# Attention scores on the tensor engine: one 64 x 128 tile per product in place of four 64 x 32 tiles

## The chip, the cores and the metric

The kernel runs on one core of a Trainium2 chip. The metric is the device time of one execution in microseconds (us), lower is better. A TensorE product ("matmul") holds one operand still in the array (its weights, brought in by a separate weight load) and streams the other past it, up to 512 columns, into a bank of PSUM. The array can be divided into tiles, so that several small products run at once.

## The reference

```
q, k, v = (x @ wqkv) split into 32 heads of 16     # x is 2048 x 512, bf16
scores  = q @ k.T / 4 ;  p = softmax(scores)       # 32 heads x 2048 x 2048
a       = (p @ v, heads joined) @ wo
b       = ((x @ w_gate) * (x @ w_up)) @ w_down     # inner width 1376
g       = sigmoid(sum(x * gate_w))
out     = g * a + (1 - g) * b
```

## The kernel before, in words

A host-side planner (`_Sched`) walks simulated time and writes out the instruction order of every engine by hand; `_Plan.emit` then adds the semaphores. Nothing is decided on the chip: each engine works through its list in order.

TensorE is used as two halves, array rows 0 to 63 (r = 0) and 64 to 127 (r = 1). The unit of work is a **group**, `pe64`: up to four matmuls of 64 rows x 32 columns side by side (`tile_position=(64 * r, 32 * cc)`, cc = 0 to 3), which together fill one half and stream the same 512 columns of time into one PSUM bank. The planner charges each group 0.216 us on its half (`s_a`, `s_d`, `v_job`, the default `slot` of `_Unit`) and picks for the two halves separately in `try_pe` and `pe_phase`, so that groups of the two halves run side by side. There are three kinds of group:

- **Scores** (`scores`, called from `s_a` and `s_d`): for one chunk of 512 queries and one block of 128 keys, the 128 keys are the weights (`KT`) and the masked queries (`QM`) are streamed. Four matmuls have the same streamed operand and differ in their 32 keys and their 32 PSUM rows. 2,048 groups, 8,192 matmuls.
- **P times V** (`pv`, from `v_job`): the weights are V of four different heads, 16 columns and a column of ones each (17), and each of the four matmuls streams another head's exponentials. 2,092 groups; these can't be one tile, as each column strip has its own streamed operand.
- **Fills** (`fill`): projections for q, k, v, the gate and up products, the down and output products, and the gate's row. 1,576 groups, nearly all of four matmuls.

ScalarE takes the exponentials of some score banks (`exp`, L1671), VectorE does others by an integer approximation (`dpass`, L1710), and VectorE and GpSimd make scaled copies of those (`copy`, L1716 and L1717). Matmuls, evacuations and copies of several (query, key) steps are in flight together, in eight PSUM banks.

Full-array matmuls (128 x 128) come only at the start: seven warm-ups (L1954), transposes of x (L1963 and L1658, the latter from `x_turn`, four matmuls a call), and the first projections (L1978). The calls of `x_turn` lie between score groups; the planner books both halves for 0.6 us for one (`x_full`).

Of the kernel before, what the change touches and what calls it, by code (L numbers as in the profile page):

```python
# [1502 lines left out]
class _Hw:  # L1503
# [63 lines left out]
        self.ps = stack.enter_context(nc.psum_tensor("ps", [128, 8, 512], F32))  # L1567


    def pe64(self, r, mms, deps):  # L1570
        def fn(pe):
            o = None
            for dst, lhs, rhs, st, sp, cc in mms:
                o = pe.matmul(dst, lhs, rhs, start=st, stop=sp, tile_position=(64 * r, 32 * cc), skip_group_check=True)  # L1574
            return o

        return self.P.op("pe", fn, deps, "pe%d" % r)

    def scores(self, r, bank, c, b, s, kt, ci, deps):
        var = s + 2 * (ci % 2)  # L1580
        lo, hi = 64 * r, 64 * r + 64
        q = self.QM[lo:hi, (4 * c + b) % 2, var, :]
        mms = []
        for cc in range(4):
            k0 = kt * 128 + 32 * cc
            mms.append((self.ps[32 * cc : 32 * cc + 32, bank, :], self.KT[lo:hi, b, k0 : k0 + 32], q, True, True, cc))
        return self.pe64(r, mms, deps)

    def cell(self, x, lo, hi):
# [17 lines left out]
    def fill(self, u, r, i, start, stop, deps):  # L1607
        lo, hi = 64 * r, 64 * r + 64
        bank = u.bank
        kind = u.mm[0]  # L1610
        mms = []
        n = 4
        if kind == "gate":
            for cc in range(1, 4) if u.mm[1] else (0,):
                mms.append((self.ps[32 * cc : 32 * cc + 1, bank, :], self.gw[lo:hi, i : i + 1], self.xT[lo:hi, cc, i, :], start, stop, cc))
            return self.pe64(r, mms, deps)
        for cc in range(4):
            c0 = 32 * cc
            if kind in ("k", "q", "u", "g"):
                if kind == "k":  # L1620
                    b, ch = u.mm[1:]
                    w = self.wk[lo:hi, i, 128 * b + c0 : 128 * b + c0 + 32]
                elif kind == "q":
                    ch, b = u.mm[1:]
                    w = self.wq[lo:hi, i, 128 * b + c0 : 128 * b + c0 + 32]
                else:
                    ch, f = u.mm[1:]
                    if c0 >= self.FW[f]:
                        continue
                    w = (self.wu if kind == "u" else self.wg)[lo:hi, i, 128 * f + c0 : 128 * f + c0 + 32]  # L1630
                x = self.xT[lo:hi, ch, i, :]
            elif kind == "v":
                ch, tt = divmod(u.mm[1], 4)
                t0 = 128 * tt + c0
                w, x = self.xT[lo:hi, ch, i, t0 : t0 + 32], self.wv[lo:hi, i, :]
            elif kind == "do":
                c, tt = u.mm[1:]
                t0 = 128 * tt + c0
                if i < 11:
                    w, x = self.hT[lo:hi, i, t0 : t0 + 32], self.wd[lo:hi, i, :]  # L1640
                else:
                    w, x = self.OT[lo:hi, (4 * c + i - 11) % 8, t0 : t0 + 32], self.wo[lo:hi, i - 11, :]
            else:
                t0 = 128 * u.mm[1] + c0
                w = self.OT[lo:hi, (12 + i) % 8, t0 : t0 + 32]
                x = self.wo[lo:hi, i, :] if i < 3 else self.wq[lo:hi, 0, :]
            mms.append((self.ps[c0 : c0 + 32, bank, :], w, x, start, stop, cc))
        return self.pe64(r, mms, deps)


# [531 lines left out]
```

## Time and profile before

| | us |
|---|---|
| median of 3 runs | 699.54 (692.03 to 699.86) |
| profiled execution, its own time | 705.51 |
| its span, first to last instruction | 703.7 |
| PE busy, weight loads busy | 682.0, 393.0 |
| ACT, DVE, POOL busy | 660.0, 624.5, 545.3 |

PE is TensorE's matmuls, PEld its weight loads, DVE VectorE, ACT ScalarE, POOL GpSimd. A row of the groups gives line, engine, operation, output and inputs, shape and count, then the busy time, the mean duration of one in ns, and the idle time before them with what ended it. `64*32 64x512` is a product with weights of 64 rows and 32 columns that streams 512 columns. All groups of four have line 1574, that of `pe64`. The end of a matmul is modelled, so its duration (about 0.38 us) is longer than the time after which the next one can follow; the spacing of the starts tells the throughput. A row of the timeline gives start, length, engine, what it is and how many such instructions were merged into it.

### The profile page before, as it was taken

How to read it: one execution, taken by the hardware profiler on the slowest of the kernel's cores; microseconds unless marked ns; L12 is line 12 of the kernel's file. 1: busy time of each engine (PE TensorE's matmuls, PEld its weight loads, DVE VectorE, ACT ScalarE, POOL GpSimd, SP SyncE). 2: the span in 40 equal slices, each digit the busy share in tenths (PEclk: the TensorE clock that was granted, in tenths of full speed). 3: DMA queues.
4: the chain of work that ended last, by engine and by line, in shares of the span. 5: the costliest groups of instructions: out<-in, count | busy, mean ns of one | idle time of the engine just before them, and what ended most of it. 6: DMA issues, size and time to landing. Idle time of an engine off the chain costs nothing.

```text
span 703.7 us, 49393 instructions
## 1 busy us (share of the span) xinstructions
PE 682.0 (97%) x22839; PEld 393.0 (56%) x22839; DVE 624.5 (89%) x1008; ACT 660.0 (94%) x1040; POOL 545.3 (77%) x617
## 2 busy tenths in 40 slices
PE   8999999999999999999997999999999999999997
PEld 5566555455465565555653566545554565556564
DVE  7889989899898879999998888999899878999985
ACT  5899999999899999999997999999999999999995
POOL 3455988788989889998997667879799877772790
PEclk9999999999999999999999999999999999999999
DMA  9101422001310010101010010100101010010101
GB/s 180 45 5 29 112 66 65 13 9 32 85 36 19 23 33 18 30 6 36 6 24 23 20 43 13 36 4 13 28 10 38 13 27 30 12 28 12 37 8 46
DMA packets 32126, 23.06 MB, mean 33 GB/s; under 512 B 17356, under 2 KB 28524, under 8 KB 31920
## 3 DMA queue, kind: packets, MB, share of 16 engines
q1 hardware_dynamic: 30784, 18.86, 10.6%
q8 instruction: 178, 2.92, 1.8%
q0 software_dynamic: 176, 0.53, 0.5%
q10 hardware_dynamic: 960, 0.52, 0.3%
q14 instruction: 28, 0.23, 0.1%
HBM read 12.23 MB, written 2.36 MB: 21 GB/s over the span
## 4 chain that ended last, share of the span: by engine, by line
PE 92%; DVE 4%; issue 2%; POOL 1%; ACT 0%; DVEq 0%; POOLq 0%; ACTq 0%
PE ps L1574 92%; DVE DB L1710 1%; DVE OT L1869 1%; POOL DB L1717 1%; PE ps L1978 0%; DVE io L1880 0%; ACT wu L1671 0%; PE ps L1963 0%; DVE hT L1848 0%; ACT wd L1671 0%; POOL wk L1717 0%; DVE wk L1710 0%; DVE gden L1697 0%; DVE ident L1885 0%; DVE qraw L1732 0%
## 5 line engine op out<-in xcount | busy, mean ns | idle before, releaser
L1574 PE MATMUL ps<-QM,KT 64*32 64x512 bf16 x8192 | 560.1, 379 | 6.9 <-DVE wk L1710 3.6
L1717 POOL INT64_ADD DB<-DB x402 | 362.5, 917 | 94.8 <-PE ps L1574 36.4
L1710 DVE TENSOR_SCALAR DB<-ps 128x512 int16<-128x512 f32 x595 | 391.4, 690 | 42.2 <-PE ps L1574 38.0
L1671 ACT ACTIVATE PT<-ps 128x512 bf16<-128x512 f32 (+1 forms) x574 | 376.8, 749 | 11.4 <-PE ps L1574 10.3
L1574 PE MATMUL ps<-DB,Vs 64*17 64x512 bf16 x3448 | 320.3, 377 | 2.6 <-issue 1.8
L1574 PEld LDWEIGHTS ps<-QM,KT 64*32 64x32 bf16 x8192 | 196.2, 90 | 153.0 <-DVE DB L1710 39.2
L1574 PE MATMUL ps<-PT,Vp 64*17 64x512 bf16 x1478 | 221.3, 377 | 1.5 <-issue 1.4
L1671 ACT ACTIVATE xT<-ps 128x512 bf16<-128x512 f32 (+1 forms) x288 | 205.5, 779 | 10.3 <-PE ps L1574 8.8
L1574 PE MATMUL ps<-xT,Vp 64*17 64x512 bf16 x784 | 144.2, 377 | 0.8 <-issue 0.6
L1574 PE MATMUL ps<-DB,Vp 64*17 64x512 bf16 x1200 | 123.5, 377 | 0.7 <-issue 0.6
L1574 PE MATMUL ps<-xT,wg 64*32 64x512 bf16 x1376 | 121.4, 377 | 1.1 <-ACT wd L1671 0.9
L1574 PE MATMUL ps<-xT,wu 64*32 64x512 bf16 x1376 | 120.7, 377 | 0.0
L1574 PEld LDWEIGHTS ps<-DB,Vs 64*17 64x17 bf16 x3448 | 92.2, 87 | 35.2 <-issue 8.7
L1574 PE MATMUL ps<-wd,hT 64*32 64x512 bf16 x1408 | 104.7, 380 | 0.0
L1671 ACT ACTIVATE wd<-ps 128x512 bf16<-128x512 f32 (+1 forms) x101 | 66.1, 740 | 3.4 <-PE ps L1574 2.8
L1717 POOL INT64_ADD wv<-DB x65 | 56.1, 869 | 14.1 <-PE ps L1574 8.5
L1574 PEld LDWEIGHTS ps<-PT,Vp 64*17 64x17 bf16 x1478 | 56.3, 86 | 14.3 <-issue 3.5
L1574 PEld LDWEIGHTS ps<-xT,wg 64*32 64x32 bf16 x1376 | 39.8, 92 | 17.9 <-PE ps L1574 2.2
L1574 PE MATMUL ps<-wv,Vs 64*17 64x512 bf16 x472 | 48.8, 376 | 0.0
L1717 POOL INT64_ADD DB<-wk x46 | 42.4, 936 | 7.5 <-DVE wk L1710 6.8
L1574 PEld LDWEIGHTS ps<-xT,wu 64*32 64x32 bf16 x1376 | 39.4, 92 | 15.1 <-issue 2.7
L1574 PEld LDWEIGHTS ps<-wd,hT 64*32 64x32 bf16 x1408 | 37.5, 93 | 11.2 <-issue 1.5
(115 smaller groups left out, 873.3 us busy)
## 6 DMA issues: line engine op xcount, KB each, us to landing
rb<-rscr SPq DMA_DIRECT2D x16, 256.0 KB
QM<-qraw SPq DMA_DIRECT2D x124, 16.0 KB, 2.3
oc<-oraw SPq DMA_DIRECT2D x60, 32.0 KB, 2.0
out_dram<-ost SPq DMA_DIRECT2D x12, 128.0 KB, 1.9
wd<-in_B_w_down_dram SPq DMA_DIRECT2D x10, 128.0 KB, 2.5
wu<-in_B_w_up_dram SPq DMA_DIRECT2D x12, 96.0 KB, 2.8
wg<-in_B_w_gate_dram SPq DMA_DIRECT2D x12, 96.0 KB, 2.6
OT<-in_A_x_dram SPq DMA_DIRECT2D x2, 256.0 KB, 4.5
```

Of the source, the lines that this page charges most:

```text
L1574: o = pe.matmul(dst, lhs, rhs, start=st, stop=sp, tile_position=(64 * r, 32 * cc), skip_group_check=True)
L1671: return self.P.op("act", lambda a: a.activation(dst, src, ACT.Exp, scale=self.ES), deps)
L1710: return self.dve(lambda v: v.tensor_scalar(dst, src, self.YB, 0.0, ALU.add, ALU.max), deps)
L1717: return self.P.op("pool", lambda e: e.int64_add(o.bitcast(I64), a.bitcast(I64), 32 * v * 0x0001000100010001), deps)
L1869: return self.dve(lambda v: v.tensor_tensor(self.OT[:, bi % 8, :], self.oc[:], self.rb[:], ALU.mult), deps)
```

## The change

The scores' loop over column strips gets a step: with `SW = 128` it makes one matmul of 64 rows x 128 columns, at column strip 0, in place of four of 64 x 32. `PW = 32` is the same kind of step for the fills, and at 32 it leaves their matmuls as they were. `pv` isn't touched. The planner, its prices, the order of the groups and all other engines' work are untouched too.

```diff
+    SW, PW = 128, 32
+
     def scores(self, r, bank, c, b, s, kt, ci, deps):
...
-        for cc in range(4):
-            k0 = kt * 128 + 32 * cc
-            mms.append((self.ps[32 * cc : 32 * cc + 32, bank, :], self.KT[lo:hi, b, k0 : k0 + 32], q, True, True, cc))
+        for c0 in range(0, 128, self.SW):
+            k0 = kt * 128 + c0
+            mms.append((self.ps[c0 : c0 + self.SW, bank, :], self.KT[lo:hi, b, k0 : k0 + self.SW], q, True, True, c0 // 32))
         return self.pe64(r, mms, deps)
...
     def fill(self, u, r, i, start, stop, deps):
-        for cc in range(4):
-            c0 = 32 * cc
+        for c0 in range(0, 128, self.PW):
+            n = self.PW
...
-                    w = self.wk[lo:hi, i, 128 * b + c0 : 128 * b + c0 + 32]
+                    w = self.wk[lo:hi, i, 128 * b + c0 : 128 * b + c0 + n]
...
-                    if c0 >= self.FW[f]:
+                    n = min(n, self.FW[f] - c0)
+                    if n <= 0:
                         continue
...
-            mms.append((self.ps[c0 : c0 + 32, bank, :], w, x, start, stop, cc))
+            mms.append((self.ps[c0 : c0 + n, bank, :], w, x, start, stop, c0 // 32))
```

More of the change, by code (lines that the diff above doesn't have):

```diff
@@ L1611, in fill @@
         mms = []
-        n = 4
         if kind == "gate":
@@ L1621, in fill @@
                     b, ch = u.mm[1:]
-                    w = self.wk[lo:hi, i, 128 * b + c0 : 128 * b + c0 + 32]
+                    w = self.wk[lo:hi, i, 128 * b + c0 : 128 * b + c0 + n]
                 elif kind == "q":
                     ch, b = u.mm[1:]
-                    w = self.wq[lo:hi, i, 128 * b + c0 : 128 * b + c0 + 32]
+                    w = self.wq[lo:hi, i, 128 * b + c0 : 128 * b + c0 + n]
                 else:
                     ch, f = u.mm[1:]
-                    if c0 >= self.FW[f]:
+                    n = min(n, self.FW[f] - c0)
+                    if n <= 0:
                         continue
-                    w = (self.wu if kind == "u" else self.wg)[lo:hi, i, 128 * f + c0 : 128 * f + c0 + 32]
+                    w = (self.wu if kind == "u" else self.wg)[lo:hi, i, 128 * f + c0 : 128 * f + c0 + n]
                 x = self.xT[lo:hi, ch, i, :]
@@ L1634, in fill @@
                 t0 = 128 * tt + c0
-                w, x = self.xT[lo:hi, ch, i, t0 : t0 + 32], self.wv[lo:hi, i, :]
+                w, x = self.xT[lo:hi, ch, i, t0 : t0 + n], self.wv[lo:hi, i, :]
             elif kind == "do":
@@ L1639, in fill @@
                 if i < 11:
-                    w, x = self.hT[lo:hi, i, t0 : t0 + 32], self.wd[lo:hi, i, :]
+                    w, x = self.hT[lo:hi, i, t0 : t0 + n], self.wd[lo:hi, i, :]
                 else:
-                    w, x = self.OT[lo:hi, (4 * c + i - 11) % 8, t0 : t0 + 32], self.wo[lo:hi, i - 11, :]
+                    w, x = self.OT[lo:hi, (4 * c + i - 11) % 8, t0 : t0 + n], self.wo[lo:hi, i - 11, :]
             else:
                 t0 = 128 * u.mm[1] + c0
-                w = self.OT[lo:hi, (12 + i) % 8, t0 : t0 + 32]
+                w = self.OT[lo:hi, (12 + i) % 8, t0 : t0 + n]
                 x = self.wo[lo:hi, i, :] if i < 3 else self.wq[lo:hi, 0, :]
-            mms.append((self.ps[c0 : c0 + 32, bank, :], w, x, start, stop, cc))
+            mms.append((self.ps[c0 : c0 + n, bank, :], w, x, start, stop, c0 // 32))
         return self.pe64(r, mms, deps)
```

## The prediction

> **What bounds the kernel now.** I read the page's totals first, then the chain that ended last, then the kinds of matmul, and then the stretches.
>
> ```profile
> span 703.7 us, 49393 instructions
> PE 682.0 (97%) x22839; PEld 393.0 (56%) x22839; DVE 624.5 (89%) x1008; ACT 660.0 (94%) x1040; POOL 545.3 (77%) x617
> PEclk9999999999999999999999999999999999999999
> PE 92%; DVE 4%; issue 2%; POOL 1%; ACT 0%; DVEq 0%; POOLq 0%; ACTq 0%
> L1574 PE MATMUL ps<-QM,KT 64*32 64x512 bf16 x8192 | 560.1, 379 | 6.9 <-DVE wk L1710 3.6
> ```
>
> The chain is 92% PE. The changed products are a good third of all matmuls (8,192 of 22,839), and weight loads are busy only 56% of the span, so there is no shortage of loads as such. The clock is granted in full. The busy time of 97% says little, as ends are modelled. How full the array really is comes from the spacing of the starts, in the timeline of the matmuls alone:
>
> ```profile
> 299.77 0.39 PE L1574 MATMUL ps<-xT,wg 64*32 64x512 bf16 x4
> 299.82 0.39 PE L1574 MATMUL ps<-DB,Vp 64*17 64x512 bf16 x4
> 299.99 0.39 PE L1574 MATMUL ps<-xT,wg 64*32 64x512 bf16 x4
> ...
> 300.20 0.39 PE L1574 MATMUL ps<-QM,KT 64*32 64x512 bf16 x4
> 300.25 0.39 PE L1574 MATMUL ps<-DB,Vs 64*17 64x512 bf16 x4
> 300.42 0.39 PE L1574 MATMUL ps<-xT,wg 64*32 64x512 bf16 x4
> 300.47 0.55 PE L1574 MATMUL ps<-QM,KT 64*32 64x512 bf16 x8
> 300.69 0.39 PE L1574 MATMUL ps<-DB,Vs 64*17 64x512 bf16 x4
> 300.85 0.39 PE L1574 MATMUL ps<-xT,wu 64*32 64x512 bf16 x4
> ...
> 301.71 0.39 PE L1574 MATMUL ps<-QM,KT 64*32 64x512 bf16 x4
> 301.77 0.39 PE L1574 MATMUL ps<-DB,Vs 64*17 64x512 bf16 x4
> 301.93 0.39 PE L1574 MATMUL ps<-QM,KT 64*32 64x512 bf16 x4
> 301.98 0.39 PE L1574 MATMUL ps<-PT,Vp 64*17 64x512 bf16 x4
> ```
>
> Two streams are braided here, one for each half of the array. On one half the groups start at 299.77, 299.99, 300.20 and 300.42, so a group takes (300.42 - 299.77) / 3 = 0.217 us; I use 0.216. On the other they start about 0.05 later, at 299.82, 300.25, 300.47, 300.69. The reader is to see that a score group (QM,KT) nearly always runs beside a P-times-V group or a fill of the other half. The array does two groups per 0.216 us, and the kinds are thoroughly mixed.
>
> The stretches give the rest of the frame (us, then busy time and count of PE, PEld, DVE, ACT, POOL, then clock):
>
> ```profile
> 0.00:10.60 10.60, 8.55 (x59) 6.22 (x59) 6.11 (x23) 3.94 (x6) 6.41 (x12) 1.00 0.91 184
> 10.60:698.70 688.10, 672.82 (x22775) 386.71 (x22772) 615.77 (x982) 655.38 (x1034) 538.88 (x605) 1.00 0.12 30
> 698.70:703.70 5.00, 0.58 (x16) 0.11 (x8) 2.67 (x4) 0.69 (x1) 0.00 (x0) 0.96 0.31 105
> ```
>
> There are 10.6 us of prologue, 688.1 us of groups and 5.0 us of tail. The program has 5,716 groups, half of them on each half of the array: 5,716 / 2 x 0.216 = 617.3 us. So some 71 us of the middle stretch aren't streaming. About 14 of these come from the order, since a half at times waits for the other one's turn in the single instruction list, and about 56 are waits.
>
> **The change part by part.**
>
> *Instructions.* 8,192 score matmuls and as many weight loads become 2,048 each; the total goes from 22,839 to 16,695. Each group still streams 512 columns into one bank, so its 0.216 us on its half stay. Weight loads lie beside matmuls before (56% busy), so fewer of them are worth nothing as long as they stay beside. Nothing moves on any other engine or queue: no DMA, no semaphore, no step. The fills at PW = 32 are the same matmuls. All of that is one term of 0.
>
> *Two tile shapes in one stream.* Before, every group of the middle stretch has 32-column tiles. After, 64 x 128 tiles stand among 64 x 32 ones. The trace of before has no 64 x 128 tile, so the nearest rows are those where `x_turn` (L1658), with 128 x 128 tiles, stands between score groups. First the matmuls of that place, then the weight loads, then the durations of these transposes:
>
> ```profile
> 11.48 0.67 PE L1658 MATMUL ps<-ident,OT 128*128 128x128 bf16 x8
> 12.30 0.41 PE L1574 MATMUL ps<-QM,KT 64*32 64x512 bf16 x8
> 12.64 0.40 PE L1658 MATMUL ps<-ident,OT 128*128 128x128 bf16 x4
> 12.97 0.40 PE L1574 MATMUL ps<-QM,KT 64*32 64x512 bf16 x4
> ```
>
> ```profile
> 11.15 0.10 PEld L1574 LDWEIGHTS ps<-QM,KT 64*32 64x32 bf16 x4 [0.37 <-DVE KT L1993]
> 11.48 0.50 PEld L1658 LDWEIGHTS ps<-ident,OT 128*128 128x128 bf16 x8 [0.23 <-issue]
> 12.64 0.23 PEld L1658 LDWEIGHTS ps<-ident,OT 128*128 128x128 bf16 x4 [0.23 <-issue]
> ```
>
> ```profile
> L1658 PE MATMUL ps<-ident,OT x16: 219/219/247, 10.3 to 12.8; 128*128 128x128 bf16 x16
> ```
>
> From the score pair at 12.30 to the score group at 12.97 are 0.67 us. In it stream one slot of scores (the pair runs on both halves at once), 0.216 us, and four transposes of 128 columns, a quarter of 0.216 each, another 0.216. What is left, 0.67 - 0.43 = 0.24, pays for two changes of shape and some 0.02 us in which the eight score matmuls are issued: 0.11 us a change. The single group at 11.15 says the same: the next shape starts at 11.48, 0.33 later, or 0.216 + 0.114. The weight loads show what happens. Inside one shape the next weights are loaded while the current matmul streams, as for the score group of 300.20, whose loads start 0.15 us ahead of it:
>
> ```profile
> 300.05 0.10 PEld L1574 LDWEIGHTS ps<-QM,KT 64*32 64x32 bf16 x4
> ```
>
> At the two changes of shape the first load of the new shape starts together with its matmul, after 0.23 us in which the loader waited for nothing that the profile shows ("issue"). So at a change of shape the array runs empty before anything of the new shape is let in.
>
> If 64 x 128 against 64 x 32 counts as a change of shape like that, two costs follow.
>
> First, **exclusion**: a score group can no longer run beside a group of another kind. I went through the order in which the planner writes PE's groups and cut it into runs of scores only and of other kinds only. There are 1,539 runs of scores: 1,157 of them are a single group, 261 are of two, 116 of three and 5 longer. They alternate with as many runs of other groups. Each run takes 0.216 us times the larger of its counts on the two halves. Summed over all runs, that is 4,137 slots in place of the 2,858 of perfect pairing: 4,137 x 0.216 = 893.6 us.
>
> Second, **the change itself**: about 3,074 boundaries between scores and other groups x 0.11 = 338 us.
>
> *What hides it, and what is late next.* Nothing hides it: PE is the chain. ACT's 660 us and DVE's 624.5 us are below the 1,232 us of these two terms, so neither becomes the bound. The waits of before shrink, since producers get almost twice the time for each group:
>
> ```profile
> PEld ps L1574 <- DVE DB L1710: 41.8, 177, 0.9
> PEld ps L1574 <- issue: 36.7, 88, 1.5
> ```
>
> They are short (41.8 / 177 = 0.24 us each), about the price of two changes of shape. I keep 15 of the 56 us; the bounds are 0 and 56.
>
> *Sum.* 10.6 + 893.6 + 338 + 15 + 5.0 = 1,262 us of span. The profiled execution took 705.51 us for its span of 703.7, so 1.8 lie around it: 1,264, say **1,265 us**. That is made against 705.51; the median of the runs shown is 699.54, 6 us lower, which is far below what is uncertain here. The forecast's own range: at 0.10 a change and no waits 10.6 + 893.6 + 307 + 5 + 1.8 = 1,218; at 0.115 and all 56 us of waits 10.6 + 893.6 + 353.5 + 56 + 6.8 = 1,320. From below, the cost of the unseen shape change is bounded by no change at all: the rows are of a tile that needs both halves, and so had to wait for both in any case.
>
> [...]
>
> **The rivals.**
>
> *A. The widths live side by side; nothing happens.* A 64 x 128 tile needs only its own half, and the two halves already run different operands at once (300.20 and 300.25). Against it: the loads of `x_turn` were held back although loads are otherwise taken early. Exclusion and price are then zero and the time is 705.5 - 6 = 700 us by the median. It decides as soon as a switch costs under 14 / 3,074 = 5 ns (14 us being 2% of 700), with pairing kept. Its better end: a quarter of the score instructions is left, and if all 36.7 us of "issue" before the loads went away, the time would be 703.7 - 36.7 + 1.8 = 669 us. That would be faster; nothing in the rows says that this idle time is due to the number of instructions.
>
> *B. Each half changes shape by itself.* The other half then goes on. In the planner's order half 0 goes 1,187 times between scores and others, half 1 1,163 times. With perfect overlap the middle takes 617.3 + 1,187 x 0.11 = 748 us; if every stop of one half also holds the other through the single list, 617.3 + 2,350 x 0.11 = 876 us. With the ends and the waits of before (10.6 + 56 + 6.8 = 73) at the lower one that is 821, and without the waits at the upper one 893; I take 850. For it: a 64 x 128 tile doesn't touch the other half's rows. Against it: at 12.30 both halves had ended together, so the rows can't tell.
>
> *C. Exclusion, but no time for the change itself.* If the 0.11 us were the price of a change between 128 and 64 rows, and a change of width only keeps the halves from overlapping: 10.6 + 893.6 + 15 + 6.8 = 926 us.
>
> **How the numbers follow.** I give the forecast 0.60, C 0.09, B 0.12, A without gain 0.12, A with a gain 0.03, and 0.04 to something above 1,330. The range leaves out A and what lies above: 820 to 1,330 holds about 0.8. The forecast's own range is 1,218 to 1,320. A measurement of this kernel can tell about 2% from no change. Faster by more than that is A's better end, 0.03; within it, A, 0.12; slower is all the rest, 0.85.
>
> **What would show it right or wrong.** The score row should read `64*128`, 2,048 times. In the timeline, a score group should start about 0.33 us after the last group of another kind began, and likewise the other way, and no score should start within 0.2 us of another kind on the other half. Nearly every such weight load should have idle time with "issue" before it. The busy sums of ACT and DVE should stay near 660 and 624 us while their shares fall to about half. If score and other groups still start 0.05 us apart, the exclusion is wrong. If they keep apart but at 0.22, the 0.11 is. If the gaps name DVE or ACT instead of "issue", I have overlooked a wait; and if the granted clock falls where it was full, the slots of 0.216 are too short.

## The result and the profile after

| us | before | after |
|---|---|---|
| median | 698.97 (4 runs) | 1,432.28 (4 runs, 1,420.58 to 1,482.43) |
| profiled execution, its own time | 705.51 | 1,427.65 |
| span | 703.7 | 1,425.9 |
| mean granted TensorE clock | 0.997 | 0.844 |

The ratio is 2.048, 95% interval 2.026 to 2.070. One of the four runs after, of 1,482.43 us at a mean clock of 0.805, is slower than the other three (1,420.58 to 1,436.91) and is left out of the ratio. The forecast was 1,265, with a range of 820 to 1,330. The direction came as forecast, and so did the two costs that it names, exclusion and the change of shape; but the median lies 102 us above the upper end, for a reason that the forecast did not price.

The page of the changed kernel, the lines that answer to those shown of before:

```profile
span 1425.9 us, 37105 instructions
PE 1418.6 (99%) x16695; PEld 357.8 (25%) x16695; DVE 654.7 (46%) x1008; ACT 734.1 (51%) x1040; POOL 546.0 (38%) x617
PEclk9998589999697685999855599999985556999999
PE 99%; DVE 1%; ACT 0%; DVEq 0%; issue 0%; ACTq 0%
L1576 PE MATMUL ps<-QM,KT 64*128 64x512 bf16 x2048 | 702.8, 432 | 0.4 <-ACT wu L1673 0.3
L1576 PEld LDWEIGHTS ps<-QM,KT 64*128 64x128 bf16 x2048 | 149.3, 95 | 577.4 <-issue 392.0
```

The instructions are as told: 2,048 score matmuls of 64 x 128, 16,695 in all. The chain is PE even more than before. The new thing is the clock row: it was 9 in every slice, and now has long stretches of 5. The timeline of the matmuls, at full clock:

```profile
599.75 0.39 PE L1576 MATMUL ps<-wk,Vs 64*17 64x512 bf16 x4
600.07 0.39 PE L1576 MATMUL ps<-QM,KT 64*128 64x512 bf16 x1
600.39 0.39 PE L1576 MATMUL ps<-DB,Vs 64*17 64x512 bf16 x4
600.40 0.40 PE L1576 MATMUL ps<-xT,wu 64*32 64x512 bf16 x4
600.73 0.39 PE L1576 MATMUL ps<-QM,KT 64*128 64x512 bf16 x1
601.05 0.40 PE L1576 MATMUL ps<-xT,wu 64*32 64x512 bf16 x4
601.38 0.39 PE L1576 MATMUL ps<-QM,KT 64*128 64x512 bf16 x1
```

The braid of two streams is gone. At 600.39 and 600.40 two groups with 32-column tiles still run side by side on the two halves. Each score stands alone: the next group starts 0.32 us later, whichever half it is on. That is 0.216 of streaming and 0.10 for the change of shape. In a stretch at low clock the same pattern is wider, 0.54 us from a score to the group behind it (749.81 to 750.35, 751.31 to 751.85):

```profile
749.81 0.61 PE L1576 MATMUL ps<-QM,KT 64*128 64x512 bf16 x1
750.35 0.60 PE L1576 MATMUL ps<-DB,Vs 64*17 64x512 bf16 x4
...
751.31 0.61 PE L1576 MATMUL ps<-QM,KT 64*128 64x512 bf16 x1
751.85 0.59 PE L1576 MATMUL ps<-xT,Vp 64*17 64x512 bf16 x1
```

Two waits of the weight loader and of DVE tell who now waits for whom (total, times, longest):

```profile
PEld ps L1576 <- issue: 798.7, 2488, 0.8
DVE DB L1712 <- PE ps L1576: 555.1, 497, 9.2
```

The loader's idle time names nobody, as at the transposes before, and DVE waits for PE. The stretches (us, then busy time and count of PE and PEld, then the clock, the DMA share and GB/s) show a clock of 1.00 or of 0.50, and the clock's record in this trace has no third value:

```profile
187.00:363.00 176.00, 176.00 (x2428) 49.21 (x2431) 1.00 0.07 18
702.00:821.00 119.00, 118.93 (x760) 21.34 (x756) 0.50 0.03 7
1061.00:1203.00 142.00, 141.93 (x934) 25.06 (x930) 0.50 0.02 6
1204.00:1420.00 216.00, 216.00 (x3407) 62.38 (x3399) 1.00 0.05 13
```

### The profile page after: what moved, and what is told of

Same layout as the page of the kernel before. It is cut to its first block, busy times and chain, and to the rows that moved or that the text cites. A ratio compares the mean times of both kernels' runs of the same rounds, so it can differ in the third digit from the quotient of the medians.

```text
span 1425.9 us, 37105 instructions
## 1 busy us (share of the span) xinstructions
PE 1418.6 (99%) x16695; PEld 357.8 (25%) x16695; DVE 654.7 (46%) x1008; ACT 734.1 (51%) x1040; POOL 546.0 (38%) x617
## 4 chain that ended last, share of the span: by engine, by line
PE 99%; DVE 1%; ACT 0%; DVEq 0%; issue 0%; ACTq 0%
PE ps L1576 99%; DVE io L1882 0%; DVE xT L1743 0%; PE ps L1980 0%; PE ps L1965 0%; DVE hT L1850 0%; DVE ident L1887 0%; DVE qraw L2000 0%; ACT QM L1993 0%; DVEq L87 0%; DVE hT L1847 0%; ACT QM L1994 0%; DVE PT L1909 0%; DVE io L1883 0%; DVE ident L1879 0%
## 5 line engine op out<-in xcount | busy, mean ns | idle before, releaser
L1576 PE MATMUL ps<-QM,KT 64*128 64x512 bf16 x2048 | 702.8, 432 | 0.4 <-ACT wu L1673 0.3
L1712 DVE TENSOR_SCALAR DB<-ps 128x512 int16<-128x512 f32 x595 | 412.6, 695 | 556.1 <-PE ps L1576 555.1
L1673 ACT ACTIVATE PT<-ps 128x512 bf16<-128x512 f32 (+1 forms) x574 | 406.3, 719 | 375.6 <-PE ps L1576 371.3
L1576 PE MATMUL ps<-DB,Vs 64*17 64x512 bf16 x3448 | 362.3, 430 | 0.0
L1576 PEld LDWEIGHTS ps<-QM,KT 64*128 64x128 bf16 x2048 | 149.3, 95 | 577.4 <-issue 392.0
L1576 PE MATMUL ps<-PT,Vp 64*17 64x512 bf16 x1478 | 247.3, 427 | 0.1
L1576 PE MATMUL ps<-xT,Vp 64*17 64x512 bf16 x784 | 165.0, 433 | 0.0
L1576 PE MATMUL ps<-DB,Vp 64*17 64x512 bf16 x1200 | 131.6, 430 | 0.1
L1576 PE MATMUL ps<-wd,hT 64*32 64x512 bf16 x1408 | 131.1, 434 | 0.0
L1576 PE MATMUL ps<-xT,wu 64*32 64x512 bf16 x1376 | 131.1, 403 | 0.0
L1576 PE MATMUL ps<-xT,wg 64*32 64x512 bf16 x1376 | 130.7, 404 | 0.0
L1576 PEld LDWEIGHTS ps<-DB,Vs 64*17 64x17 bf16 x3448 | 77.4, 86 | 134.3 <-issue 113.2
L1712 DVE TENSOR_SCALAR wk<-ps 128x512 int16<-128x512 f32 (+1 forms) x59 | 41.2, 700 | 56.7 <-PE ps L1576 56.5
L1576 PEld LDWEIGHTS ps<-PT,Vp 64*17 64x17 bf16 x1478 | 52.0, 86 | 56.8 <-issue 47.9
L1719 POOL INT64_ADD wk<-DB x43 | 38.5, 899 | 50.3 <-PE ps L1576 26.3
L1712 DVE TENSOR_SCALAR wv<-ps 128x512 int16<-128x512 f32 x52 | 35.9, 690 | 43.8 <-PE ps L1576 43.7
L1576 PE MATMUL ps<-wv,Vs 64*17 64x512 bf16 x472 | 51.8, 429 | 0.0
```

Of the source, the lines that this page charges most:

```text
L1673: return self.P.op("act", lambda a: a.activation(dst, src, ACT.Exp, scale=self.ES), deps)
L1712: return self.dve(lambda v: v.tensor_scalar(dst, src, self.YB, 0.0, ALU.add, ALU.max), deps)
L1719: return self.P.op("pool", lambda e: e.int64_add(o.bitcast(I64), a.bitcast(I64), 32 * v * 0x0001000100010001), deps)
```

## The experiments

Theory after the result: the shape changes cost what was forecast, about 1,218 us of work at full clock, and the rest is the clock, which is halved when too little of the array is fed. Rivals for the clock: it falls through the changes themselves, or because few matmul instructions are issued. Rival for the work: the wide product is dear by itself.

**Patterns alone.** Only TensorE works (one run of this program, and one of the second), in loops such as

```diff
+            for n in range(100):            # pattern D
+                group(pe, "D", 0, n, 32)
+                group(pe, "D", 1, n, 32)
+                group(pe, "D", 0, n, 128)
+                group(pe, "D", 1, n, 128)
```

> This kernel leaves the reference's work out: it only issues patterns of groups on TensorE, 60 us or so of each, with some 11 us of dense 64x32 groups ahead of each, and writes one PSUM bank out. N is a group of four 64x32 tiles, W one 64x128 tile, a and b the halves. Theory: any change of width costs 0.10 us on top of the 0.216, and keeps even tiles of different halves from overlapping; the clock falls by how little of the array streams per window, below about 12 groups of 31 possible per 3.4 us. Expected spacing of starts: A (Na Nb dense) 0.108 us a group; B (Na alone) 0.216; C (Na, Wb) 0.32 a group at full clock, and the clock falls; D (Na Nb Wa Wb) 0.32 a pair, full clock; E (Wa Wb) 0.108, full clock; F (Na, 64x64 pair on b) like C; G (one 64x32 tile alone) 0.216, an eighth of the array; H (Wa alone) 0.216, full clock; K (Na, Wa on the same half) like C; L (128x128) 0.216, full clock; M (three pairs N, one W) 1.06 us a round, full clock. Rival 1, the clock falls through the changes themselves (9 or 10 a window in the trace): it falls in C, D, F and K and stays up in B, G, H, L. Rival 2, it falls when few matmul instructions are issued (26 to 30 a window in the trace): it falls in G, H and L (16 a window) and not in D (54). If the clock goes by area, G falls; if by the time in which anything streams, G stays up.

The stretches, in the order A, B, C, D, E, F, G, H, K, L, M (length, PE busy and count, clock):

```profile
22.00:87.00 65.00, 61.51 (x2192) 1.00 0.02 4
100.00:159.00 59.00, 59.00 (x1105) 1.00 0.01 2
178.00:275.00 97.00, 97.00 (x454) 0.50 0.00 1
289.00:353.00 64.00, 64.00 (x970) 1.00 0.01 2
366.00:425.00 59.00, 59.00 (x550) 1.00 0.01 1
444.00:542.00 98.00, 98.00 (x534) 0.50 0.00 1
558.00:616.00 58.00, 58.00 (x270) 1.00 0.00 1
629.00:688.00 59.00, 59.00 (x275) 1.00 0.00 1
707.00:803.00 96.00, 96.00 (x445) 0.50 0.00 1
818.00:876.00 58.00, 57.74 (x265) 1.00 0.00 1
889.00:953.00 64.00, 64.00 (x1475) 1.00 0.01 3
```

The clock falls in C, F and K and in no other. D has ten matmuls a round: 97 rounds in 64 us, 0.66 us each, 0.33 for a pair of groups. So D makes as many changes per time as C would at full clock, and keeps the clock: rival 1 falls. G, H and L issue one matmul per 0.215 to 0.219 us (58 / 270, 59 / 275, 58 / 265), 16 in 3.4 us and fewer than the changed kernel's 26, and keep it: rival 2 falls. G, an eighth of the array, keeps it as well, so the theory's word "area" was wrong: the width of a tile made no difference here (64 x 32 in G, 64 x 128 in H, both at 1.00). What C, F and K share is that two 64-row halves together are fed two thirds of one half's time. C at half clock has five matmuls for two groups, 97 / (454 / 5) / 2 = 0.534 us a group. K, where both shapes are on the same half, is as slow (96 / (445 / 5) / 2 = 0.539): which half the tiles are on made no difference.

**The measure of the clock, more closely.**

> Patterns again, without the reference's work. On half a: A two N then one W, B three and one, C five and one, D eight and one; E one 32x32 tile alone, F one 32x128 tile alone, G two 32x128 tiles of different rows at once, H pairs as in D of the first patterns, but each N with one of its four strips alone. Theory, the clock goes by fed rows times time, counted in groups of 64 rows x 512 columns per 3.4 us, whatever the columns, and falls below about 12: A has 12.0 (open), B 12.8, C 13.7, D 14.3 and stay at full clock; E and F have 7.9 and fall; G has 15.8 and H 21 and stay. Rival, time in which anything streams: E, F stay like G; H like the pairs. Rival, area of the array: H has 62% of a quarter and a half, 42% of the array, and G 50%, F 25%, E 6%: E falls, but a 64x32 tile with 12.5% alone stayed up.

```profile
22.00:81.00 59.00, 59.00 (x621) 1.00 0.01 1
93.00:152.00 59.00, 59.00 (x719) 1.00 0.01 2
164.00:223.00 59.00, 59.00 (x829) 1.00 0.01 2
235.00:294.00 59.00, 59.00 (x915) 1.00 0.01 2
311.00:421.00 110.00, 110.00 (x259) 0.50 0.00 0
441.00:549.00 108.00, 108.00 (x255) 0.50 0.00 0
562.00:622.00 60.00, 60.00 (x560) 1.00 0.01 1
634.00:696.00 62.00, 62.00 (x390) 1.00 0.00 1
```

These are A to H. A 32-row tile streaming without a pause loses the clock with 32 columns (E) and with 128 (F). Two 32-row tiles at once (G) keep it, as one 64-row tile with 32 columns did (G of the first). H keeps it with one strip of four in its N groups. So in these patterns rows fed times time count, and the width of the tiles doesn't. In groups of 64 rows x 512 columns per 3.4 us, A with 12.0 keeps the clock and C of the first patterns, 3.4 / 0.32 = 10.7, loses it. The window of 3.4 us was taken from the clock's record in the trace of the changed kernel, where for instance stretches at half clock last 58.0, 119.5 and 143.4 us, or 17, 35 and 42 times 3.413; the one in the kernel before (below) lasts 3.413 us. The price of a change comes out here too: A has nine matmuls a round, 59 / (621 / 9) = 0.855 us, or three slots of 0.216 and two changes of 0.10; B 59 / (719 / 13) = 1.067, four slots and two changes of 0.10.

The traces of the kernels themselves agree. They can be cut into windows of 3.413 us at the edges of the clock's record, and the streaming in each be counted, at 0.216 us a group at full clock and 0.425 at half (pattern E, 110 / 259). In the changed kernel the six windows ahead of a fall hold 10.5 to 11.7 groups, and the six ahead of a rise 11.6 to 13.1. None of the 276 others at full clock holds under 11.4 (median 16.3), and none of the 124 others at half clock over 11.7 (median 7.7). So the limit lies near 11.5 in both directions, and half clock keeps itself going: pattern C, with 10.7 groups in a window at full clock, brings 3.413 / 0.534 = 6.4 into one at half clock, so the clock comes back only at a much denser stretch of the order, here behind the six windows of 11.6 to 13.1. Changes of shape aren't needed for a fall: the batched order with 64 x 32 tiles alone (below) has none, and its clock falls twice, each time behind a window of 10.3 groups.

**The same order with the rows fed.**

```diff
-            mms.append((self.ps[c0 : c0 + self.SW, bank, :], self.KT[lo:hi, b, k0 : k0 + self.SW], q, True, True, c0 // 32))
-        return self.pe64(r, mms, deps)
+            return pe.matmul(self.ps[:, bank, :], self.KT[:, b, k0 : k0 + 128], q, start=True, stop=True, skip_group_check=True)
```

> The same order, but each score product is one 128x128 tile: it also streams the queries of the other half through the keys of the other half, so the scores are sums over the heads of both halves and the output isn't the reference's. Changes of shape as before (3,073); score groups can't pair any more, which makes 975 us of slots in place of 894. Theory: the clock goes by the rows that are fed, a score now counts as two groups, and about 20 groups' worth fall into 3.4 us, so the clock stays full: 975 + 307 + 17 = 1,300 us at clock 0.99 to 1.0. Rival, the clock falls through the changes of shape, or because single matmuls are issued: it falls as much as in the changed kernel or more, 1,430 to 1,560 us.

It took 1,326.74 us, ratio to before 1.879 (1.861 to 1.897):

```profile
core 0: 1325.6 us, clock 0.999
```

This kernel does more on TensorE than the changed one and has the same 3,073 changes, yet it is about 100 us faster, and its clock stays full: counted as above, with a score as two groups, no window between prologue and end holds under 13.0 (a lower bound, as some of its score matmuls are missing in the trace). The theory's 1,300 was 27 us short.

**A quarter of the scores wide.**

```diff
+        sw = self.SW if kt % 4 == 0 else 32
```

> Only the scores of every fourth key block are 64x128 tiles, the others stay four of 64x32. The same order then has 3,306 slots and 965 changes. Theory: 714 + 96.5 + 17.4 for the ends = 828 us and up to half of the waits of before, so 830 to 860, at full clock, since about 16 groups fall into 3.4 us on the average. Rival, a price for each wide product whatever stands beside it: a quarter of the whole rise, 699 + 733 / 4 = 882.

848.08 us, ratio 1.201 (1.194 to 1.208), clock full:

```profile
span 847.9 us, 46321 instructions
PEclk9999999999999999999999999999999999999999
```

The count of slots and changes in the order with the ends, 828 us, tells the time to 2.4%, and the rival's 882 falls. Counted in the same way, no window between prologue and end holds under 12.9 groups.

**Two tiles of 64 x 64 per score.** The edit is `SW = 64`.

> Scores as two tiles of 64x64 in place of one of 64x128. The order has the same 4,136 slots and 3,073 changes. Theory: any other width than the neighbours' is a change of shape, so 1,218 us of work at full clock and, with the clock falling as before, about 1,430. If the clock goes by the number of matmul instructions, there are 2,048 more and the loss is smaller: 1,220 to 1,350. If only 128 columns (the undivided width) need the array empty, about 700.

1,552.79 us at a mean clock of 0.779 in one run and 1,581.85 in the other, which was profiled. Even the first is at least 8% slower than with 128 columns, not about equal; the idea that more instructions hold the clock falls again. The profiled one:

```profile
core 0: 1580.1 us, clock 0.762
```

A boundary to 64 x 64 is a change of shape too, and a little dearer: pattern F, with six matmuls for two groups, takes 98 / (534 / 6) / 2 = 0.551 us a group at half clock where C takes 0.534. The array is then fed a little less still. That this is why the clock was lower here fits, but wasn't tried by itself.

**Fills wide as well.** The edit is `PW = 128`.

> Scores and fills as 64x128 tiles, P times V still 64x32. The order then has 4,859 slots and 3,983 changes. Theory: 1,050 + 398 + 17 = 1,465 us at full clock, with 13.5 groups in 3.4 us on the average, so nearer to the 12 at which the clock falls: half clock for some 60% of the time, 1,465 / (1 - 0.6 x 0.485) = 2,070, range 1,700 to 2,300. Rival, it is something about the score products alone: about 1,430 as before.

2,326.72 us at a mean clock of 0.564 in one run, a little above the range, and 2,394.95 in the other, which was profiled:

```profile
core 0: 2392.2 us, clock 0.543
```

The scores are not special: more boundaries, with the fills, cost more. The clock was down for 2 x (1 - 0.564) = 87% of the time in the first run and 91% in the second, in place of the 60% that I had put in. That 60% went by the average at full clock, 13.5 groups in 3.4 us. At half clock the median window of this trace holds 7.5, and the clock came back only behind windows of 12.2 to 14.0.

**The planner told of the shapes.** Each place that issues a group first asks this, so that scores come in runs:

```diff
+    def shape(self, m):
+        if m == self.mode:
+            return True
+        t = max(self.hf) + self.CH
+        if self.mode is not None and t > self.now + 1e-9:
+            self.at(t)
+            return False
+        self.mode = m
+        return True
```

> 64x128 scores, but the planner knows of the shapes: a group of the other shape is issued only when both halves are idle and 0.11 us have passed, so it forms runs. Slots 3,908, changes 739 in place of 3,073. Theory: 844 + 74 + 17.4 = 935 us at full clock if nothing waits, up to the planner's own 1,012 with waits; the clock stays full, with 20 groups in 3.4 us. Rival, the wide product itself is dear (0.36 us each, whatever the order): about 1,400 again.

> The order of the batched planner, with scores as four 64x32 tiles. No change of shape. Theory: 792 us of slots in that order and 17 of ends, 810 to 900 with waits, clock full. The distance to the batched kernel with 64x128 tiles (1,021) is then what shape costs in that order: 52 us of exclusion and 739 changes at 0.10, 126 us. Rival, wide products are dear by themselves: the distance is 2,048 x 0.2 us or more, over 300 us.

The first took 1,020.95 us, ratio 1.446 (1.441 to 1.451), at a clock of 0.992. It is 1.4 times as fast as the changed kernel with the same tiles, and nearly at full clock; the rival's 1,400 falls. It is 9 us above the upper end of what was expected. With 64 x 32 tiles the same order took 976.73, ratio 1.383 (1.368 to 1.399), well above the expected 810 to 900. So this order waits a lot by itself (first with 64 x 128 scores, then with 64 x 32):

```profile
ACT xT L1695 <- PE ps L1598: 220.1, 93, 17.6
...
PEld ps L1598 <- issue: 118.4, 332, 0.8
PEld ps L1598 <- PE ps L1598: 116.0, 334, 0.6
```

```profile
ACT xT L1695 <- PE ps L1598: 197.9, 80, 18.3
...
PEld ps L1598 <- ACT xT L1695: 77.1, 192, 1.0
PEld ps L1598 <- ACT PT L1695: 60.0, 151, 1.0
```

With wide tiles the loader's longest waits are for nothing that the profile names ("issue") and for PE, with narrow ones for ACT: 77.1 + 60.0 = 137 us, against 46.6 + 32.5 = 79 us for ACT with wide tiles. The two differ by 44 us only, not 126. That fits a price of shape which in part falls into time in which PE would have waited anyway, but it wasn't tried by itself. The rival's 300 us fall in either case. No version here beats the kernel before.

## Why the prediction was wrong, point by point

- **Instructions at 0:** right. 16,695 of them, and the other engines have the same instructions; ACT and DVE were busy 51% and 46% of the span. One sign that the prediction named did not hold: ACT's busy time rose from 660.0 to 734.1 us. Its instructions did not get longer. Before, 409 exponentials with a mean of 632 ns were counted as 221.7 us busy, less than 409 x 0.632 = 258, so they overlapped; after, with 596 ns, they make 239.8, nearly 409 x 0.596 = 244.
- **Exclusion, 893.6 us:** right. No row of before has a 64 x 128 tile beside a 64 x 32 one; that the pair counts as a change of shape was my assumption, and that the array runs empty at a change was read off 0.23 us in which the loader stood still. What the runs measured is the distance of the starts: over the 3,072 boundaries in the trace's middle stretch no group starts less than 0.30 us from one of the other width, and the count of slots, with the changes, gave the time of the wide quarter to 2.4%. Rival A (side by side) falls by that timeline. Rival B (each half by itself) falls by pattern C: there neither half ever changes its own width, yet a group takes 0.534 us at half clock, where two halves that don't hinder each other would issue one per 0.425 / 2.
- **The change itself, 0.11 us:** nearly right; it is 0.10 in the timeline and in A and B of the second patterns. 3,074 of them make 307 us, not 338. Rival C (no price) falls with it.
- **Waits, 15 us of 56:** not refuted, but not measured by itself. ACT and DVE wait for PE now, and the account below leaves 1 to 2% for everything not counted.
- **The failed step: "The clock is granted in full".** That was read off the kernel before and carried over to the kernel after. Every slot of 0.216 us rested on it. The exclusion which the prediction itself derived leaves one group at a time in most of the stream. The average is still 16 groups in 3.4 us (5,716 in 1,218 us), but where single scores alternate with single groups it is 10.7, and the patterns put the limit between 10.7 and 12.0. In its place the runs showed a mean clock of 0.844, which by the account below cost about 189 us. The prediction named a falling clock only among the signs at its end, and gave it neither a price nor a place in the range.

The sentence wasn't quite true of the kernel before either. Behind a pause of PE of 3.63 us, up to 379.33 us, its clock was at one half for one window of 3.4 us (us, PE busy and count, clock, DMA share, GB/s):

```profile
375.60:379.00 3.40, 0.10 (x4) 1.00 0.00 0
379.00:382.40 3.40, 3.06 (x64) 0.50 0.00 0
```

The row of 9s hides this: a slice of 17.6 us with 3.4 us at half clock averages 0.90. Only the mean clock of 0.997 and the 3.6 us of idle time in the row of the scores hint at it.

The size of it: at full clock the work is 10.6 + 893.6 + 307 + 5.0 + 1.8 = 1,218 us. At half clock a slot takes 0.425 (pattern E of the second kernel, 110 us / 259) and a change about 0.11 (C: 0.534 - 0.425), so all of it would take 893.6 x 0.425 / 0.216 + 338 + 17 = 2,113 us. A mean clock of 0.844 means half clock for 2 x 0.156 = 31.2% of the span, 445 us, in which 445 / 2,113 = 21% of the work is done; in the other 981 us 981 / 1,218 = 81%. Together 102%, so with the measured clock put in, clock and shape account for the time to 2%. The 445 us at half clock did work that takes 0.21 x 1,218 = 256 us at full clock, so the clock cost 189 us; the other 19 of the 208 us between 1,218 and 1,426 are waits or errors of the counts. Two other runs fit the same account: for their clocks of 0.848 and 0.838 it gives 1,398 and 1,412, and 1,420.58 and 1,436.91 were measured, 1.6% and 1.8% more. So does the kernel with wide fills: 4,859 slots and 3,983 changes make 1,465 us at full clock and 1,050 x 0.425 / 0.216 + 438 + 17 = 2,521 at half, which for its clock of 0.564 gives 2,307, and 2,326.72 was measured.

No pause like the 3.63 us of the kernel before stands ahead of the falls in the changed kernel: in its stream of groups (L1576) the weight loader's longest wait was 0.8 us, and the windows of 3.413 us ahead of a fall held 10.5 to 11.7 groups each. Pattern E of the second patterns, a 32-row tile streaming without a pause, lost the clock as well.

## What to carry to other kernels

In these runs 64 x 128 tiles among 64 x 32 ones cost 0.10 us at each boundary and stopped the halves of the array from running side by side (64 x 64 tiles did much the same, at half clock 0.551 us a group against 0.534), so narrow tiles that match their neighbours were cheaper than one wide tile that doesn't. Before pricing a change that thins the stream, count what it leaves in each 3.4 us, not only on the average: below about 12 groups of 64 rows x 512 columns the clock itself halved here, fewer groups then fit into the same time, and a slot's price taken from the kernel before no longer holds. A count of slots and boundaries in the issue order gave the time to 2 or 3% where the clock stayed up and PE was what bounds the kernel (1,300 against 1,326.74, 828 against 848.08); where other engines set the pace, it did not.

## What the runs showed of the hardware that was not expected

In the patterns the clock went by the rows that are fed, not by the width of the tiles or their area: one 64 x 32 tile, an eighth of the array, streams for 58 us at full clock, while a 32 x 128 tile alone, a quarter of it, falls to 0.50; a pair of 32 x 128 tiles stays up for 60 us. A boundary between 64 x 32 and 64 x 64 tiles cost as much as one to 64 x 128, or slightly more (0.551 against 0.534 us a group at half clock). And not every difference in width was a change of shape: 64 x 17 and 64 x 32 groups start side by side before and after the change (300.25 and 300.20, 600.39 and 600.40), and with wide fills so do 64 x 96 and 64 x 128 tiles:

```profile
583.79 0.63 PE L1576 MATMUL ps<-xT,wu 64*96 64x512 bf16 x1
583.79 0.63 PE L1576 MATMUL ps<-QM,KT 64*128 64x512 bf16 x1
```
